# Windowed attention and expert choice on one core: one mask-and-maximum product for three blocks, and a single search over both halves of the key for the first list

## Chip, cores and metric

The kernel runs on 1 core of one Trainium2 chip. The metric is the device time of one execution in microseconds (us). The kernel before took 684.95 us, the median of three runs (682.93 to 686.85).

## The reference

Attention over 8 batches and 8 heads of 576 tokens, head size 64. Heads 0 to 3 see the last 32 positions, heads 4 to 7 every fourth of the last 128. Its result, 4608 tokens of 512 numbers, goes through a mixture of 8 experts: all (token, expert) logits are sorted, and each pair is accepted in that order while the token is free and the expert has under 576 tokens.

```python
scores = scale * np.matmul(q, k.transpose(0, 1, 3, 2))
scores = np.where(masks[None, :, :, :], scores, -1000000000.0)
scores = scores - np.max(scores, axis=-1, keepdims=True)
attn = np.exp(scores)
attn = attn / (np.sum(attn, axis=-1, keepdims=True) + 1e-09)
x = np.matmul(attn, v)            # as (B*S, H*D)
logits = x @ w_gate
order = np.argsort(-logits.flatten())
for idx in order:
    tok, e = (int(idx) // E, int(idx) % E)
    if assigned[tok] >= 0 or counts[e] >= cap:
        continue
    assigned[tok] = e
    counts[e] += 1
for e in range(E):
    out[assigned == e] = np.maximum(x[assigned == e] @ w1[e], 0.0) @ w2[e]
```

## The kernel before

**Attention.** There are 32 units: batch b, kind (plain or dilated heads) and ui (a pair of heads). A unit has 9 blocks c of 64 queries, in two halves h of 32; a half sees 64 keys. `Unit.build` (L434) makes its work:
- `scan` (L491): the mask by a product with the identity (L494) and bf16 scores on top of it (L498), into a PSUM tile pm, in two groups of 5 and 4 blocks (`gr`, L423). DVE takes each row's maximum into mx (L445).
- The turn (L450): one product with the identity turns mx, so that 9 rows hold the maxima; DVE copies them as bf16 into rows 64 to 72 of the unit's tile in R (L452). The rows above hold fixed choosers (`rsel`, loaded by `choosers`, L363).
- `scores` (L501), three times three blocks: for each block and half one product of `lsel` (mask rows and -1 for the maximum) with R (L505, 73 rows, 64 columns), then the fp32 scores on top (L510). ACT takes the exponential into E (L464).
- `values` (L514): E times V (L522); `weigh` (L526) on DVE divides by the sums into xs. `banks` (L567) turns xs (L581) and ACT copies it into xt; per batch the gate's logits follow (L606, L627).

The work is not issued in program order: `Schedule` (L155) is given each operation's cost, dependencies and due time, and a planner writes down one order for each engine when the kernel is built. On the chip each engine takes its instructions in that order and waits for semaphores. All loads are issued on SP's queue and are held back until PE has come to a mark (`paced`, L317); the constants and the first unit's loads come first (L740 to L750).

**Lists.** `choose` (L927) makes, as tokens are finished, each token's largest logit, its expert (oh0) and a sortable key, of which V0 holds the upper 16 bits and `lo` the lower; `bits` (L933) writes the expert as a bit into who; `coarse` (L798) counts keys over 256 thresholds. An expert's list closes at the first key for which it has 576 tokens. `alone` (L949) finds this for the first list with no other work beside it: `search_alone` (L870) runs rounds of flags on DVE (L825, L827), counts of 36 chunks on PE (L892), the comparison with 576 (L905) and a product that hands the step to all rows (L906); twice over the upper half (the coarse counts spare two rounds), then `low` (L976) builds V2 from the found place (L908) and the lower half, and four rounds follow over V2. Then the expert's bit (L963), the number of tokens above the found key in each expert (`over`, L967), the flags of members (L972), `ranks` (L1070: sums over all rows and over earlier rows, L1074 and L1075), `expert` (L1018: one-hot, what is still open, and the index eidx for the loads), `need_of` (L1054: how many tokens of equal key fit), and `accept` (L1077: running sums L1082, places, acceptance). `slots` and `listing` (L1302) turn the places into a list of token numbers: digits on DVE (L1128), their product with the chunk number on GpSimd (`by_chunk`, L1132) and with the row number on ACT, and PE's placing (L1153); `indices` (L1156) makes idx.

**Experts.** Round r: GpSimd gathers the list's tokens from DRAM in five tiles (L1332), PE turns them (L1346), ACT and DVE split them into high and low parts, three products for each block form the hidden layer (L1383) and the output (L1426), GpSimd scatters the rows. The next lists (`search`, L1251; `settle`, L1276) are made beside it. `fetch` (L1461) reads eidx on SP, and behind it the expert's w1 blocks are loaded (L1226); from the fourth on they wait for a mark that GpSimd writes after the gathers (L1217).

## Time and profile before

| | us |
|---|---|
| median of 3 runs | 684.95 |
| the profiled execution | 684.68 |
| its span, first to last instruction | 682.7 |
| PE busy, PE weight loads | 627.5, 548.3 |
| DVE, ACT, GpSimd busy | 463.4, 295.1, 207.0 |

Columns of a row: start and duration in us, engine, source line, operation, written tile <- read tiles, size, count, and in brackets the engine's idle time ahead of it and what ended it. PE is the product, PEld its weight load, POOL is GpSimd, SPq the sequencer of the load queue. The view of busy time by stage gives PE, PEld, DVE, ACT and POOL in this order and ends its rows with PE's granted clock (1.00 is full), the busy share of the 16 DMA engines and GB/s. A busy PE is not a PE at its peak, since products overlap. In the chain of work that ended last PE has 54% of the span, DVE 18%, and 15% is "issue", time for which the profile names no releaser.

### The profile page before, as it was taken

To read this page: it belongs to the slowest core of one execution; us is meant where nothing else is said; L and a number is where in the kernel's file an instruction comes from. 1 tells how busy PE (TensorE), PEld (TensorE's weight loads), DVE (VectorE), ACT (ScalarE), POOL (GpSimd) and SP (SyncE) were. 2 spreads that over 40 slices of the span, in tenths; PEclk is the share of its full clock that TensorE was granted. 3 is DMA by queue.
4 is the path that set the end of the run, shared out by engine and by line. 5 is a ranking of instruction groups with operands and counts; after the bars stand their busy time and mean duration, and the time that the engine had idled before them with its cause. 6 is when DMAs were issued, how large, how long until landed. Compare 5 with 4: busy or idle time off the path is not lost.

```text
span 682.7 us, 19041 instructions
## 1 busy us (share of the span) xinstructions
PE 627.5 (92%) x7514; PEld 548.3 (80%) x7514; DVE 463.4 (68%) x1576; ACT 295.1 (43%) x644; POOL 207.0 (30%) x316
## 2 busy tenths in 40 slices
PE   7889886789856999999999999999999999999994
PEld 5777776678644988998799799889879979988983
DVE  6677756876677885689798598778869736614200
ACT  5645453455403835855345145335423526424210
POOL 5465566552004217524113113110320311311011
PEclk9999999999957999999999999999999999999998
DMA  8998798872204937967236117214513644202001
GB/s 245 281 270 261 186 254 246 242 203 69 73 1 153 237 66 202 275 142 252 92 96 208 42 56 228 90 55 139 178 48 88 238 170 147 70 31 102 1 28 42
DMA packets 51674, 99.10 MB, mean 145 GB/s; under 512 B 7168, under 2 KB 17152, under 8 KB 51584
## 3 DMA queue, kind: packets, MB, share of 16 engines
q1 hardware_dynamic: 42240, 72.71, 35.5%
q0 software_dynamic: 9344, 25.17, 13.4%
q8 instruction: 59, 0.97, 0.6%
q14 instruction: 31, 0.25, 0.1%
HBM read 72.69 MB, written 18.87 MB: 134 GB/s over the span
## 4 chain that ended last, share of the span: by engine, by line
PE 54%; DVE 18%; issue 15%; DMA 5%; POOL 4%; ACT 2%; POOLq 0%; SPq 0%; DVEq 0%; ACTq 0%
PE ph L1383 16%; PE py L1426 16%; PE px L522 4%; PE pS L510 3%; PE px L581 2%; DVE xs L532 2%; PE ptx L1346 2%; POOL xg L1332 1%; DVE hb L1404 1%; POOL out L1452 1%; PE pz L813 1%; DVE mx L445 1%; DVE G L827 1%; PE py L1429 1%; PE py L1431 1%
## 5 line engine op out<-in xcount | busy, mean ns | idle before, releaser
L1426 PE MATMUL py<-w2h,hb 128*128 128x512 f32 x512 | 170.5, 398 | 0.0
L1383 PE MATMUL ph<-xh,w1h 128*128 128x256 f32 (+1 forms) x512 | 138.3, 301 | 0.0
L1383 PE MATMUL ph<-xh,w1l 128*128 128x256 f32 (+1 forms) x512 | 136.3, 297 | 0.0
L1383 PE MATMUL ph<-xl,w1h 128*128 128x256 f32 (+1 forms) x512 | 136.1, 296 | 0.0
L1426 PEld LDWEIGHTS py<-w2h,hb 128*128 128x128 f32 x512 | 96.1, 188 | 19.1
L1208 ACT ACTIVATE hb<-ph 128x256 fp32r<-128x256 f32 (+2 forms) x192 | 59.7, 346 | 102.4 <-PE ph L1383 100.5
L1452 POOL DMA_INDIRECT out<-y,idx x40 | 40.4, 1011 | 209.2 <-ACT y L1208 145.5
L1426 PE MATMUL py<-w2l,hb 128*128 128x512 f32 x256 | 99.8, 390 | 0.0
L1383 PEld LDWEIGHTS ph<-xh,w1h 128*128 128x128 f32 x512 | 91.7, 189 | 0.6
L1383 PEld LDWEIGHTS ph<-xl,w1h 128*128 128x128 f32 x512 | 91.6, 189 | 0.0
L1383 PEld LDWEIGHTS ph<-xh,w1l 128*128 128x128 f32 x512 | 91.5, 190 | 0.0
L1404 DVE SCALAR_TENSOR_TENSOR hb<-ph,hb 128x320 fp32r<-128x320 f32 (+1 forms) x128 | 57.1, 453 | 34.1 <-ACT hb L1208 30.6
L464 ACT ACTIVATE E<-pS 128x384 f32<-128x384 f32 x96 | 46.1, 490 | 54.3 <-PE pS L510 49.2
L1208 ACT ACTIVATE y<-py 128x512 f32<-128x512 f32 (+1 forms) x40 | 23.9, 597 | 96.0 <-PE py L1426 83.2
L510 PE MATMUL pS<-q,k 128*64 128x64 f32 x1152 | 54.2, 230 | 4.6 <-issue 4.6
L1426 PEld LDWEIGHTS py<-w2l,hb 128*128 128x128 f32 x256 | 48.2, 188 | 8.5
L1332 POOL DMA_INDIRECT xg<-xd,idx x40 | 41.6, 1039 | 36.3 <-PE ph L1383 26.2
L522 PE MATMUL px<-v,E 128*64 128x65 f32 x1152 | 47.7, 224 | 4.5 <-issue 2.2
L522 PEld LDWEIGHTS px<-v,E 128*64 128x64 f32 x1152 | 42.1, 138 | 8.4 <-issue 4.8
L297 POOL COPY v<-v 32x520 f32<-32x520 f32 (+2 forms) x56 | 33.4, 620 | 50.3 <-DMA v<-in_vd 20.7
L1209 DVE TENSOR_TENSOR xl<-ptx,xh 128x512 fp32r<-128x512 f32 (+1 forms) x36 | 22.9, 636 | 36.7 <-ACT xh L1208 28.7
L510 PEld LDWEIGHTS pS<-q,k 128*64 128x64 f32 x1152 | 45.3, 141 | 2.9 <-issue 2.9
(203 smaller groups left out, 1118.7 us busy)
## 6 DMA issues: line engine op xcount, KB each, us to landing
raw<-in_moe_w SPq DMA_DIRECT2D x128, 256.0 KB
qs<-in_qp SPq DMA_DIRECT2D x16, 288.0 KB
k<-in_kp SPq DMA_DIRECT2D x16, 288.0 KB
qs<-in_qd SPq DMA_DIRECT2D x16, 288.0 KB
k<-in_kd SPq DMA_DIRECT2D x16, 288.0 KB
xd<-xs SPq DMA_DIRECT2D x8, 512.0 KB
w2l<-raw POOLq DMA_DIRECT2D x16, 256.0 KB
v<-in_vp SPq DMA_DIRECT2D x8, 325.0 KB
```

The costliest lines, as they stand in the source:

```text
L297: f(t[:32, c0 + 1:c1 + 1], t[96:, c0:c1])
L464: e = self.op("ACT", 490, lambda j=j, pS=pS: nc.scalar.activation(self.E[:, 3 * j:3 * j + 3].rearrange("p c x -> p (c x)"), pS.tile[:, :38 ...
L510: x = nc.tensor.matmul(pS[64 * h:64 * h + 64, k, :, h], self.K[:, 32 * g:32 * g + 64], self.Q[:, g], start=False, stop=True, skip_group_ch ...
L522: x = nc.tensor.matmul(px[64 * h:64 * h + 64, c - c0, a], self.E[:, k, 64 * a:64 * a + 64], self.V[:, k, 2 * self.ui + a], start=True, sto ...
L532: nc.vector.tensor_tensor(xs[:, c0:c1, 2 * self.ui:2 * self.ui + 2], px[:, :m, :, :D], rc[:, :, :, None].to_broadcast([128, m, 2, D]), op= ...
L1208: act = lambda o, i, f=AF.Copy: nc.scalar.activation(o, i, f)
L1209: sub = lambda e, o, a, b: e.tensor_tensor(o, a, b, op=OP.subtract)
L1332: nc.gpsimd.indirect_dma_start(out=xg[:n], out_offset=None, in_=xd, in_offset=bass.IndirectOffsetOnAxis(ap=box[0][:n, m:m + 1], axis=0))
L1383: nc.tensor.matmul(o, a[:, d * 128:d * 128 + 128], b[:, d, c0:c1], start=((d, i) == pairs[0]), stop=((d, i) == pairs[-1]))
L1404: hl = op("DVE", 335 if j == 0 else 400, lambda: nc.vector.scalar_tensor_tensor(hb[:, CAP + c0:CAP + c1], o, 0.0, hb[:, c0:c1], op0=OP.max ...
L1426: nc.tensor.matmul(py, x, w, start=(f + i == 0), stop=(f == NF - 1 and i == 2))
L1452: s = nc.gpsimd.indirect_dma_start(out=out, out_offset=bass.IndirectOffsetOnAxis(ap=box[0][:n, m:m + 1], axis=0), in_=y[:n], in_offset=None)
```

## The change

*Attention.* `lsel` and `rsel` are laid out anew: three blocks stand in rows 0 to 95 and the nine maxima in rows 96 to 104, so that one product of 192 columns for each half (instead of three of 64) gives mask and maximum of three blocks. For that the maxima are written into three column sets of a wider mx, turned by three products, and copied (9 rows, 384 wide) into the wider R by ACT instead of DVE. The groups of the maxima become 6 and 3 blocks. R is loaded in two parts, one for each kind, from one copy in DRAM; mask tables are a third smaller.

*First list.* `search_alone` becomes one loop of six rounds: in its fourth the step is handed on in units of 65536 and X = 65536 (V0 - base) + lo replaces V0, so that found and `low` go. `bits` of the last five chunks moves from the attention's end into a round of that loop. `over` and `need_of` go; need is 576 less the last running sum (`accept`). A third product in `ranks` with -1024 on the diagonal makes the place of accepted tokens negative, in place of an addition. In the first list the product with the chunk number runs on DVE, between the digits, not on GpSimd; `named` (the open experts and eidx) is split off `expert` and put behind the last digits, and the fetch of eidx with the w1 loads behind it follows. The copies for the next search (`copies`) wait for the second gathered tile. Tiles of the gather and rx are touched ahead of the search.

*Later lists.* `count` counts once instead of twice, and `need_of` is gone.

The diff, cut to its core:

```diff
-        ls = np.zeros((128, NB, 64), np.float32)
+        ls = np.zeros((128, 3, 2, 64), np.float32)
-            ls[32 * h:32 * h + 32, c] = win
-            ls[64 + c, c] = -1.0
+            ls[32 * (c % 3):32 * (c % 3) + 32, c // 3, h] = win
+            ls[96 + c, c // 3] = -1.0
-    r = np.zeros((2, 32, 4, 2, 2, 32), np.float32)
-    for h in range(2):
-        r[h, :, :, h] = np.eye(32)[:, None, None, :]
-    bf["rsel"] = np.concatenate([r.reshape(64, -1), np.zeros((64, 512), np.float32)])
+    r = np.zeros((4, 32, 3, 2, 2, 32), np.float32)
+    for k in range(3):
+        r[k, :, k] = np.eye(32)[:, None, None, :]
+    bf["rsel"] = r.reshape(128, -1)
...
-    RS = pk.tile([128, 4, 128], BF, name="R")
+    RS = pk.tile([128, 4, 3, 128], BF, name="R")
-    MX, REC = ring(pk, [128, 64], BF, "mx", 3), ring(pk, [128, LG], F32, "rec", 3)
+    MX, REC = ring(pk, [128, 256], BF, "mx", 3), ring(pk, [128, LG], F32, "rec", 3)
...
-    def choosers():
+    def choosers(kind):
         c0, w = load_const.where["rsel"]
-        return nc.sync.dma_start(RS.rearrange("p x i -> p (x i)"), T["in_cb"][:, c0:c0 + w])
+        return nc.sync.dma_start(RS[:, 2 * kind:2 * kind + 2].rearrange("p x k i -> p x (k i)"),
+                                 T["in_cb"][:, None, c0:c0 + w].to_broadcast([128, 2, w]))
...
-            self.gr, self.gv = ((0, 5), (5, 9)), ((0, 3), (3, 5))
+            self.gr, self.gv = ((0, 6), (6, 9)), ((0, 3), (3, 5))
...
-                d = self.op("DVE", 80 * (c1 - c0), lambda c0=c0, c1=c1, pm=pm: nc.vector.tensor_reduce(
-                    mx[:, c0:c1], pm.tile[:, :64 * (c1 - c0)].rearrange("p (c j) -> p c j", j=64), axis=AX.X, op=OP.max),
+                d = self.op("DVE", 170 + 64 * (c1 - c0), lambda c0=c0, c1=c1, pm=pm: nc.vector.tensor_reduce(
+                    mx[:, 32:227].rearrange("p (k x) -> p x k", x=65)[:, c0:c1:3],
+                    pm.tile[:, :64 * (c1 - c0)].rearrange("p (j k x) -> p j k x", k=3, x=64), axis=AX.X, op=OP.max),
...
-            t = self.op("PE", 60, lambda: nc.tensor.matmul(pm.tile[64:, :128], mx, C["ident"], start=True, stop=True), md, B_A)
+
+            def turn(pm=pm):
+                for k in range(3):
+                    nc.tensor.matmul(pm.tile[64:, 128 * k:128 * k + 128], mx[:, 64 * k:64 * k + 64], C["ident"],
+                                     start=True, stop=True, skip_group_check=True)
+
+            t = self.op("PE", 150, turn, md, B_A)
             usem.append(t)
-            rc = self.op("DVE", 290, lambda: nc.vector.tensor_copy(self.r[64:64 + NB], pm.tile[64:64 + NB, :128]),
-                         [t, ready["r"], *old("r", kind, ui)], B_A)
+            o = self.r[96:96 + NB].rearrange("p k x -> p (k x)")
+            deps = [t, ready["r", kind], *old("r", kind, ui)]
+            rc = self.op("ACT", 500, lambda: act(o, pm.tile[96:96 + NB, :384]), deps, B_A)
...
         def scores(self, j, pS):
             pS = pS[:, :384].rearrange("p (c a h i) -> p c a h i", c=3, a=2, h=2)
-            for k in range(3):
-                for h in range(2):
-                    nc.tensor.matmul(pS[64 * h:64 * h + 64, k, :, h], self.ls[:64 + NB, 3 * j + k], self.r[:64 + NB, 64 * h:64 * h + 64],
-                                     start=(k == 0), stop=False, skip_group_check=True)
+            for h in range(2):
+                nc.tensor.matmul(pS[64 * h:64 * h + 64, :, :, h], self.ls[:96 + NB, 2 * j + h], self.r[:96 + NB, :, 64 * h:64 * h + 64],
+                                 start=True, stop=False, skip_group_check=True)
...
-        un.op("DVE", 350, lambda: R.bits(c0 - 1, c1), [x], B_P)
...
-    ready["r"] = sp(1, choosers, (), 131000, 0)
+    ready["r", 0] = sp(1, lambda: choosers(0), (), 197000, 0)
     load(0, 0, 1)
     load_values(0, 0)
+    ready["r", 1] = sp(1, lambda: choosers(1), (), 197000, 0)
     load(0, 1, 0)
...
+        big, V65 = (pw.tile([128, n], d, name=x, bufs=1) for n, d, x in ((128, BF, "unit65"), (NCH, F32, "V65")))
+        nc.scalar.activation(big, C["unit0"], AF.Copy, scale=float(NK))
+        nc.scalar.activation(self.down, C["ident"], AF.Copy, scale=-1024.0)
...
+        V, kb, base = self.V0, self.kstep(2, False), None
+        for it in range(2, 8):
+            w = kb.shape[1]
+            ps = self.pz[:w, 420:420 + NE]
...
-                self.flags(V, psc if it else None, kt, c0, c1)
+                self.flags(V, psc, kb, c0, c1)
                 for c in range(c0, c1):
                     nc.tensor.matmul(ps, self.G[:, c, :w], oh[:, c], start=(c == 0), stop=(c == NCH - 1))
+            b = pw.tile([128, 1], F32, name="base")
+            if base is None:
+                nc.vector.tensor_copy(b, psc)
+            else:
+                nc.vector.tensor_scalar(b, psc, base, 65536.0 if it == 3 else -1.0 if it == 7 else 0.0,
+                                        op0=OP.add, op1=OP.mult if it == 3 else OP.add)
+            base = b
+            if it == 2:
+                nc.vector.tensor_scalar(V65, V, 65536.0, None, op0=OP.mult)
+            if it == 3:
+                V = self.X = pw.tile([128, NCH], F32, name="X")
+                nc.vector.scalar_tensor_tensor(V, V65, base, self.lo, op0=OP.subtract, op1=OP.add)
+                kb, base = self.kstep(0, True), None
+            elif it < 7:
+                kn = self.kstep((it + 1) % 4, it > 3)
                 kb = pw.tile([128, NK + 1], F32, name="kb")[:, :kn.shape[1]]
                 nc.vector.tensor_scalar(kb, kn, base, None, op0=OP.add)
+            if it == 5:
+                self.bits(NCH - 5, NCH)
             flag = pw.tile([NK + 1, 1 + NE], BF, name="flaga")
             nc.vector.tensor_scalar(flag[:w, 1:], ps, float(CAP), None, op0=OP.is_ge, op1=OP.max, accum_out=flag[:w, :1])
-            nc.tensor.matmul(self.pa[:, :1 + NE], C[f"unit{it}"][:w], flag[:w], start=True, stop=True)
...
+            nc.tensor.matmul(self.pa[:, :1 + NE], (big if it == 3 else C[f"unit{it % 4}"])[:w], flag[:w], start=True, stop=True)
+        self.delta, self.base = psc, base
...
-        self.search_alone(self.V, self.oh, False)
-        self.low()
-        self.search_alone(self.V2, self.oh, True)
+        self.search_alone()
...
-        s = pw.tile([n, 1], F32, name="sa")
-        nc.vector.tensor_scalar(s, self.C["kpos"][:n, 1:], self.delta[:n], None, op0=OP.is_equal)
-        pr = pw.tile([n, NE], F32, name="pra")
-        nc.vector.tensor_scalar(pr, self.ps, s, None, op0=OP.mult)
-        self.over = self.pa[:, 16:16 + NE]
-        nc.tensor.matmul(self.over, self.C["onesf"][:n], pr, start=True, stop=True)
-        self.above()
+        gg = pw.tile([128, 2, NCH], BF, name="gg")
+        for w, o in ((0, OP.is_gt), (1, OP.is_equal)):
+            nc.vector.tensor_scalar(gg[:, w], self.X, self.delta, self.base, op0=OP.subtract, op1=o)
+            if w == 0:
+                bit = pw.tile([128, 1], I32, name="bit")
+                nc.vector.tensor_reduce(bit, self.fe, axis=AX.X, op=OP.max)
...
+        self.em = em
+
+    def named(self):
+
+        nc, pw, em = self.tc.nc, self.pw, self.em
...
-        nc.tensor.matmul(ps[:, 2 * NCH:], C["tri"], ge, start=True, stop=True)
+        nc.tensor.matmul(ps[:, 2 * NCH:], C["tri"], ge, start=True, stop=False, skip_group_check=True)
+        nc.tensor.matmul(ps[:, 2 * NCH:3 * NCH], self.down, ge[:, :NCH], start=False, stop=True, skip_group_check=True)
...
-        pre = self.pre = pw.tile([128, 2, NCH], F32, name="pre")
+        need = pw.tile([128, 1], F32, name="need")
+        nc.vector.tensor_scalar(need, scan[:, 0, NCH - 1:], -1.0, float(CAP), op0=OP.mult, op1=OP.add)
+        pre = pw.tile([128, 2, NCH], F32, name="pre")
         nc.vector.tensor_tensor(pre, ps[:, 2 * NCH:].rearrange("p (w c) -> p w c", w=2), scan, op=OP.add)
+        slot = self.slot = pw.tile([128, NCH], F32, name="slot")
+        nc.vector.scalar_tensor_tensor(slot, pre[:, 1], need, pre[:, 0], op0=OP.min, op1=OP.add)
         acc = self.acc = pw.tile([128, NCH], F32, name="acc")
-        nc.vector.scalar_tensor_tensor(acc, pre[:, 1], self.need, ge[:, 1], op0=OP.is_lt, op1=OP.mult)
-        nc.vector.tensor_tensor(acc, acc, ge[:, 0], op=OP.add)
+        nc.vector.scalar_tensor_tensor(acc, pre[:, 1], need, ge[:, 1], op0=OP.is_lt, op1=OP.mult)
...
-    def by_chunk(self, c0, c1):
+    def by_chunk(self, c0, c1, first):
+        if first:
+            pair = lambda x: x.rearrange("p c (x t) -> p c x t", t=2)
+            n = self.C["ctab"][:, 2 * c0:2 * c1].rearrange("p (c t) -> p c t", t=2)
+            return self.tc.nc.vector.tensor_tensor(
+                pair(self.rx[:, c0:c1, 0]), pair(self.oa[:, c0:c1]),
+                n[:, :, None, :].to_broadcast([128, c1 - c0, NM, 2]), op=OP.mult)
...
+    for x in XG.tiles:
+        nc.gpsimd.memset(x[:1, :1], 0.0)
     R.alone()
...
-            nd = st["need"] = chain("DVE", 310, R.need_of, [], B_L)
-            nd = st["need"] = chain("DVE", 310, R.need_of, [m, st.get("slots")], B_L)
...
-            oc = chain("ACT", 1055, lambda: R.copies(R.oh, nc.scalar), [lv])
+            st["left1"] = lv
+            oc = chain("ACT", 1055, lambda: R.copies(R.oh, nc.scalar), [lv]) if r else None
...
+        if r:
+            rows(*halves[0])
+        for k, n in enumerate(OB[r > 0]):
             c0, c1 = c1, c1 + n
-            lows.append((op("DVE", 100 + 36 * n, lambda c0=c0, c1=c1: R.within(c0, c1), [d], B_L), c0, c1))
-        halves = [(0, 14), (14, NCH)] if r == 0 else [(0, NCH)]
-        xs = [(op("POOL", 150 + 30 * (c1 - c0), lambda c0=c0, c1=c1: R.by_chunk(c0, c1), [d], B_L),
-               op("ACT", 250 + 9 * (c1 - c0), lambda c0=c0, c1=c1: R.by_row(c0, c1), [d], B_L)) for c0, c1 in halves]
+            if r == 0 and k < 2:
+                rows(*halves[k])
+            deps = [xs[-1][0]] if r == 0 else [d]
+            lows.append((op("DVE", 100 + 36 * n, lambda c0=c0, c1=c1: R.within(c0, c1), deps, B_L), c0, c1))
+        if r == 0:
+            st["named"] = op("DVE", 350, R.named, [lows[-1][0]], B_L + 5000)
...
+        if r == 0:
+            st["fetch"] = EN[r] = get(st["named"])
+        en = EN[r]
         X[r] = gather(r, ix, BOX[r])
+        if r == 0:
+            st["next"][0] = chain("ACT", 1055, lambda: R.copies(R.oh, nc.scalar), [st["left1"], X[0][1][0]])
```

## Rows read from the trace of the kernel before

**Rows 1.** busy time by stage: stretch, its us, each engine's busy us (count)

```profile
0.00:188.00 188.00, 158.31 (x4064) 135.82 (x4064) 133.29 (x439) 96.27 (x205) 93.66 (x161) 1.00 0.76 212
20.00:68.00 48.00, 43.41 (x1179) 38.34 (x1180) 33.09 (x107) 28.11 (x62) 28.45 (x45) 1.00 0.92 270
68.00:119.00 51.00, 39.75 (x1157) 36.24 (x1157) 33.66 (x110) 22.89 (x48) 31.68 (x52) 1.00 0.88 231
188.00:218.50 30.50, 17.69 (x306) 12.82 (x307) 23.16 (x100) 4.79 (x8) 7.11 (x8) 0.61 0.19 57
218.50:660.00 441.50, 437.56 (x3086) 388.44 (x3085) 306.90 (x1039) 192.27 (x428) 103.16 (x142) 1.00 0.43 128
```

**Rows 2.** PE's waits, 68 to 119 us: us, times, longest

```profile
PE pS L510 <- issue: 4.6, 4, 1.4
PE pS L505 <- issue: 3.6, 4, 2.0
PE px L522 <- ACT E L464: 0.8, 1, 0.8
PE pm L494 <- DVE R L452: 0.8, 1, 0.8
PE px L522 <- issue: 0.8, 1, 0.8
```

**Rows 3.** busy time between restarts of PE, columns as in rows 1

```profile
68.75:118.82 50.07, 39.58 (x1148) 36.07 (x1148) 33.66 (x110) 22.89 (x48) 30.80 (x50) 1.00 0.88 231
108.87:114.25 5.38, 3.85 (x128) 3.65 (x128) 4.19 (x12) 2.72 (x5) 3.25 (x6) 1.00 1.03 244
```

**Rows 4.** DMA queues, 106 to 107.6 us: packets, MB, share

```profile
q8 instruction: 1, 0.02, 4.0%
```

**Rows 5.** timeline of PE, 29 to 30 us

```profile
29.09 0.30 PE L494 MATMUL pm<-const 128*64 128x256 bf16 x2
29.22 0.29 PE L498 MATMUL pm<-k,q 128*64 128x64 bf16 x8
29.34 0.26 PE L505 MATMUL pS<-R,const 73*64 73x64 bf16 x6
29.44 0.55 PE L510 MATMUL pS<-q,k 128*64 128x64 f32 x12
```

**Rows 6.** groups by line, 0 to 187 us: busy us, mean ns, idle

```profile
L464 ACT ACTIVATE E<-pS 128x384 f32<-128x384 f32 x96 | 46.1, 490 | 54.3 <-PE pS L510 49.2 <-PE pm L450 4.7
...
L452 DVE CAST R<-pm 9x128 bf16<-9x128 f32 x32 | 9.3, 289 | 10.3 <-PE pm L450 8.8 <-PE px L522 0.9
```

**Rows 7.** DVE's waits, 0 to 188 us

```profile
DVE R L452 <- PE pm L450: 8.8, 13, 1.4
```

**Rows 8.** chain of work that ended last, 0 to 20 us: start, us, what

```profile
13.13 5.55 DMA v<-in_vd
```

**Rows 9.** timeline of DVE and PE, 194 to 206 us

```profile
194.24 0.22 DVE L908 TENSOR_SCALAR found<-py,base 128x1 f32<-128x1 f32 x1 [0.26 <-PE py L906]
...
195.22 0.90 DVE L825 TENSOR_TENSOR G<-V,const 128x224 bf16<-128x224 f32 x3
...
203.28 0.22 DVE L908 TENSOR_SCALAR found<-py,base 128x1 f32<-128x1 f32 x1 [0.26 <-PE py L906]
203.41 0.22 DVE L959 SCALAR_TENSOR_TENSOR fe<-py,const 128x8 f32<-128x8 f32 x1
...
204.75 0.25 PE L1075 MATMUL pz<-ge,const 128*128 128x72 bf16 x1
...
205.61 0.29 DVE L1082 TENSOR_TENSOR_SCAN scan<-const,pz 128x72 f32<-128x72 f32 x1
```

**Rows 10.** timeline of all engines, 206 to 216 us

```profile
206.69 1.48 SPq L1226 DMA_DIRECT2D raw<-in_moe_w  x3
...
211.45 1.45 POOL L1332 DMA_INDIRECT xg<-xd,idx  x1 [2.20 <-DVE idx L1165]
...
215.31 0.66 PE L1346 MATMUL py<-const,xg 128*128 128x128 f32 x4 [0.84 <-DMA xg<-xd,idx]
```

114 lines of the change are left out of this document (47 added, 67 removed).

## The prediction

> **What bounds the kernel now.** I read the busy time by stage first, to see where PE has idle time that an edit could give back. From 218.5 us on PE is busy 437.56 of 441.50 us [rows 1]: there an edit on another engine is worth nothing, but whatever makes that stretch begin earlier moves the end by as much. Two stretches ahead of it are open: the attention (up to 188 us, PE busy 158.31), and the lone search for the first list (188 to 218.5 us), where PE is busy 17.69 of 30.50 us and the instructions wait for each other one by one.
>
> Inside the attention I read PE's waits of 68 to 119 us. PE is busy 39.75 of 51 us there [rows 1], and 9.0 us of its waits, nine of them, stand under "issue", with no releaser; E and the copy into R hold it 0.8 us each [rows 2]. What the nine are shows in a window cut from one such restart to the next: it holds exactly 128 products and 128 weight loads, 256 instructions, and takes 5.4 us, in which PE is busy 3.85 [rows 3]. The DMA view just ahead of the first of these restarts (108.87 us) shows one packet of the instruction queue [rows 4]. So I read PE as waiting for the next 256 of its own instructions. The 50.07 us from 68.75 to 118.82 hold 1148 and 1148 of them [rows 3], nine blocks.
>
> The Trainium skill's Runtime: NRT & Kernel Launch, section Instruction fetch mechanics, has instructions come in blocks of 256 and says that the cost of crossing a block's edge is mostly hidden. The block's size agrees with rows 3, the hiding does not. By the page's rule the waits would have another cause and fewer instructions would give nothing, which is the first rival below.
>
> **Part 1, attention.** (a) *Scores.* Six mask-and-maximum products in each third of a unit become two with 192 columns. Six run in 29.44 - 29.34 = 0.10 us; a pair of 256 columns, one in each half of the array, takes 29.22 - 29.09 = 0.13 us [rows 5], so a pair of 192 takes 0.08 to 0.10. PE gains 0 to 0.02 us in each of 96 thirds, 0 to 1.9 us; I take 0, because the columns are the same.
> (b) *Instructions.* A unit has 18 such products; they become 6, and one turn of the maxima becomes three: 10 products and 10 loads fewer, 20 of a unit's 254 (4064 + 4064 up to 188 us, over 32 units [rows 1]), 7.9%. Where PE waits for blocks, time goes with their number: 7.9% of 50.07 us is 3.9 us. Bounds: 0, if something else is late at once, and -4.5 with a few such waits elsewhere. I take -3.5, a little under the whole, because the waits there (9.0 us) are over twice that and the transfers have room: 231 GB/s against 270 from 20 to 68 us [rows 1].
> (c) *Two more turns a unit*, 128 columns each: 0.05 us apiece at the pitch of rows 5 (0.13 us for 256), 32 x 0.10 = 3.2 us in all. In the block-bound stretch the wait hides them (some 9 units); of the other 23 about half lie on PE's path. Bounds 0 and +3.2; I take +1.1.
> (d) *The copy into R* goes from DVE (0.289 us, 32 times) to ACT, three times as wide. The nearest ACT row is the exponential of 128x384, 0.49 us [rows 6], so about 0.5 us, 16 us of ACT in all; ACT is busy 96.27 of 188 us [rows 1]. DVE loses 9.2 us of work and also the 8.8 us in which it stood before this copy, 13 times, until PE had turned the maxima [rows 7]; the weighing and the next maxima were queued behind it. ACT now stands there, with exponentials and the copies of Q and XT behind it, and PE's second product waits for the exponentials. PE itself waited 0.8 us for the copy in 51 us [rows 2], 2.9 us over 188; I take -1.2, under half, because the copy itself is longer on ACT. Bounds: -9.2 (all that DVE loses of work) and +8.4 (the third rival).
> (e) *Maxima.* 5 + 4 blocks become 6 + 3 with the same elements: 0.
> (f) *Constants.* R grows from 128 KB to twice 192 KB, both mask tables shrink by 48 KB: 160 KB more ahead of the first V of the second kind, and the chain runs through that load (5.55 us from its issue [rows 8]). At 270 GB/s [rows 1]: +0.6 us; bounds 0 (hidden) and +0.8.
> Sum: -3.5 + 1.1 - 1.2 + 0.6 = **-3.0 us**.
>
> **Part 2, the first list.** (a) *One search.* The second half's first flags start when PE's answer comes (194.24 us, where L908 starts), not at 195.22 [rows 9]: -0.98 us. V65, X and the bases run while PE counts. (b) *bits* of the last blocks moves into a later round: two instructions of some 0.2 us (the nearest is L908's 0.22 [rows 9]), where DVE waits for PE only a part of that: +0.3, bounds 0 and +0.4; where it was, DVE waited for PE anyway, so nothing comes back. Both: -0.7; bounds -1.0 and -0.5.
> (c) *Tail.* found, s, pr and their product go, and *need* comes from the running sums. Before, the sums (L1082) start at 205.61 us, 2.33 us after PE's answer (203.28), though PE's ranks ended at 205.00 (L1075: 204.75 + 0.25) [rows 9]: DVE was late, with the index and need_of. After: three instructions fewer ahead of the ranks, at a pitch of 0.13 us, the distance of L908 and L959 [rows 9]: -0.4; one more small product, +0.05; then the sums start 0.26 us behind PE, DVE's wait in L908's row. 205.00 - 0.4 + 0.05 + 0.26 = 204.91: -0.7. *need* and the dropped addition cancel.
> (d) *GpSimd out.* Two DVE products of 140 and 220 elements, about 0.2 us each, one of them ahead of the first digits; it takes the place of GpSimd's, for which PE's placing waited before: 0, bounds -0.3 and +0.3. (e) The first gather's instruction takes 1.45 us [rows 10]; a part of that may be the first use of the tiles, now touched early: -0.1, bounds -0.5 and 0.
> Gather earlier by 0.7 + 0.7 + 0.1 = 1.5 us.
> (f) *Index behind the list.* named() moves behind the last digits, some 0.4 us that PE's placing hides. The SP queue fetches the index after it, so the first three w1 blocks (768 KB), issued from 206.69 us on, well ahead of the first gather at 211.45 [rows 10], come at about the gather's own time. On SP only w1's other blocks are queued behind them, and those wait for the gathers anyway. PE needs w1 only when the gathered tokens are turned (from 215.31 us [rows 10]) and split, so its own lateness costs 0; but 768 KB take 2.8 us at 270 GB/s, beside the gathers' first 512 KB (1.9 us). Bounds: 0, and +1.9 if both gathers wait as long as they take themselves; I take +0.6, a third, since both queues move at once. (g) The copies for round 1 go behind the second tile, off the path.
> Sum: -1.5 + 0.6 = **-0.9 us**.
>
> **Part 3, later rounds.** need_of goes, one small product a list comes. PE is full: at most +0.3 us; I take 0.
>
> **Rivals.** *The blocks give nothing*: another limit (transfers, busy 0.88 of that stretch) holds PE as long, and the wait only changes its name. For it: that share. Against: 270 GB/s were moved just before. Then the attention gives +0.5 (b = 0) and the list -0.9: 684.68 - 0.4 = 684.3 us.
> *DVE was the brake*: without the copy half of its bound arrives, 4.6 us instead of 1.2: 684.68 - 3.9 - 3.4 = 677.4 us. Against: from 68 to 119 us DVE is busy 33.66 of 51.
> *ACT becomes the gate* (slower). A copy that PE waits for costs its 0.5 us and the mean wait that DVE had before it, 8.8 / 13 = 0.7 us, 1.2 together, in place of the 1.2 gained by (d). It decides from about 5 of 32 units on: 684.68 - 2.7 + 5 x 1.2 is 3.3 us over the run before. With 7, half of the 13: 684.68 - 2.7 + 8.4 = 690.4 us. For it: ACT takes its work in order and gets 16 us more. Against: ACT is busy about half, and PE waited for E once in rows 2.
>
> **How the numbers follow.** The profiled execution took 684.68 us (a span of 682.7 and 2 around it), 0.3 under the median of 684.95, so its rows stand for the runs: 684.68 - 3.0 - 0.9 = **680.8 us**. Chances: forecast 0.60 (own range 678 to 683), blocks give nothing 0.20, DVE 0.08, ACT 0.12. A measurement of this kernel tells about 0.5% (3.4 us) from no change, so faster means under 681.5: 0.42 of the forecast's 0.60, and DVE's 0.08, together 0.50. Slower: 0.11 of ACT and 0.02 of the first rival, 0.13. The rest, 0.37, is within 0.5%. The range leaves out ACT's case and a part of DVE's: 676.5 to 686.
>
> **What would show it.** Right: the experts' first product about 4 us earlier; PE's "issue" waits of that stretch down from 9.0 us to about 6, with more of a unit in a block of 256; DVE's waits for the turn gone, and ACT's before the copy short; no gap between the two halves of the search, and the sums some 1.4 us sooner. Wrong: PE waiting for E; "issue" waits as long as before; the tokens' first turn not earlier, behind the w1 blocks.

## The result and the profile after

| | us |
|---|---|
| kernel before, median of 4 | 684.18 (682.93 to 686.85) |
| changed kernel, median of 4 | 693.36 (690.22 to 695.08) |
| ratio | 1.0109 (95%: 1.0071 to 1.0147) |
| forecast | 680.8 (676.5 to 686) |

The change makes the kernel 1.1% slower; the forecast had the wrong sign and its range doesn't hold the time. Ratios, here and below, leave out disturbed executions (up to four of six, in `a_start`), so they are not always the quotient of the medians; differences in us are the ratio's distance from 1 times the median of before beside it. The profiled execution of the changed kernel took 690.22 us (span 688.3), its fastest: the profile shows 5.5 of the 9.2 us.

Busy time by stage, changed kernel, columns and stretches of [rows 1]:

```profile
0.00:188.00 188.00, 157.68 (x3698) 134.76 (x3703) 122.43 (x394) 109.76 (x235) 94.81 (x161) 0.96 0.74 210
20.00:68.00 48.00, 42.35 (x1013) 37.00 (x1015) 28.36 (x91) 30.09 (x64) 25.99 (x41) 0.93 0.87 239
68.00:119.00 51.00, 42.88 (x1044) 37.70 (x1040) 33.40 (x108) 30.52 (x68) 32.46 (x51) 0.97 0.88 248
188.00:218.50 30.50, 17.54 (x334) 12.76 (x331) 23.09 (x106) 3.28 (x10) 3.48 (x8) 0.61 0.17 50
218.50:660.00 441.50, 435.96 (x3088) 387.24 (x3089) 309.03 (x1029) 193.46 (x431) 104.41 (x143) 1.00 0.42 129
```

PE has 9% fewer products up to 188 us (the change takes away 7.9%; the rest come later than 188 us, since the attention ends later), DVE 11 us less and ACT 13.5 us more work. But PE's granted clock in the attention is 0.96 where it was 1.00, and the attention's last keys come at 191.65 us, before at 187.09. What was forecast inside it mostly came about. PE's waits of 68 to 119 us, to be set beside [rows 2]:

```profile
PE pS L518 <- issue: 2.4, 2, 1.7
PE px L530 <- issue: 2.1, 1, 2.1
PE px L614 <- issue: 2.1, 1, 2.1
```

"issue" fell from 9.0 to 6.6 us there. The copy into R, from the groups by line, 0 to 192 us:

```profile
L286 ACT ACTIVATE R<-pm 9x384 bf16<-9x384 f32 x32 | 15.5, 483 | 13.9 <-PE pm L455 6.9 <-PE px L530 2.4 <-issue 1.5
```

And PE's waits for it, same stretch (us, times, longest):

```profile
PE pS L513 <- ACT R L286: 0.8, 2, 0.6
```

0.48 us each, as estimated, and PE waits for it 0.8 us in the whole attention: ACT's copy is no gate. The list's part, timeline of all engines, beside [rows 9] and [rows 10]:

```profile
198.56 1.09 DVE L836 SCALAR_TENSOR_TENSOR G<-X,py,const 128x224 bf16<-128x224 f32 x3 [0.26 <-PE py L924]
...
206.80 0.23 DVE L974 SCALAR_TENSOR_TENSOR fe<-py,const 128x8 f32<-128x8 f32 x1 [0.26 <-PE py L924]
...
208.03 0.23 PE L1082 MATMUL pz<-ge,down 128*128 128x36 bf16 x1
...
208.29 0.30 DVE L1089 TENSOR_TENSOR_SCAN scan<-const,pz 128x72 f32<-128x72 f32 x1
...
213.66 1.48 SPq L1245 DMA_DIRECT2D raw<-in_moe_w  x3
...
214.63 1.13 POOL L1362 DMA_INDIRECT xg<-xd,idx  x1 [20.38 <-DVE Lt L1072]
...
219.45 0.91 PE L1376 MATMUL py<-const,xg 128*128 128x128 f32 x4 [2.25 <-DMA xg<-xd,idx]
```

The second half's flags follow PE's answer after 0.26 us, without a gap; the sums start 0.26 us behind the last rank's product. From the first flags (190.19 us before, 194.50 after) to the sums it was 15.42 us and is 13.79. Little of that reaches the experts: from the first flags to the first turn of gathered tokens it was 25.12 us (to 215.31) and is 24.95 (to 219.45).

What the forecast has no step for stands at the start, PE's timeline:

```profile
17.66 0.39 PE L507 MATMUL pm<-k,q 128*64 128x64 bf16 x12
20.86 1.76 PE L589 MATMUL px<-const,xs 128*128 128x128 f32 x10 [2.81 <-DMA const<-in_cf]
22.55 0.37 PE L503 MATMUL pm<-const,const 128*64 128x192 bf16 x2
```

PE turns xs (L589) before it has finished the next unit's maxima (L503), and waits 2.8 us for the identity of that turn to land; the third unit's last exponential starts at 26.74 us instead of 22.21, the fourth's at 31.29 instead of 24.80. In the kernel before, the maxima came first and the same wait was 1.05 us; in `att` and `aft`, which have the changed kernel's order and are described below, it is 2.60 and 2.13. Nothing in the diff moves these operations: the planner did, from the new costs and load sizes.

### The profile page after: what moved, and what is told of

Read it like the earlier page. It is cut to its first block, busy times and chain, and to the rows that moved or that the text cites. A ratio compares the mean times of both kernels' runs of the same rounds, so it can differ in the third digit from the quotient of the medians.

```text
span 688.3 us, 18430 instructions
## 1 busy us (share of the span) xinstructions
PE 630.7 (92%) x7201; PEld 550.6 (80%) x7203; DVE 454.6 (66%) x1528; ACT 308.9 (45%) x679; POOL 207.4 (30%) x319
## 4 chain that ended last, share of the span: by engine, by line
PE 53%; DVE 17%; issue 15%; DMA 8%; POOL 3%; ACT 3%; POOLq 0%; SPq 0%; DVEq 0%; ACTq 0%
PE ph L1413 16%; PE py L1456 16%; PE px L530 3%; DMA raw<-in_moe_w 3%; PE pS L518 3%; PE px L589 2%; PE ptx L1376 2%; PE pz L822 1%; DVE hb L1434 1%; DVE xs L540 1%; DMA v<-in_vd 1%; DVE G L836 1%; POOL out L1482 1%; PE py L1459 1%; DVE mx L446 1%
## 5 line engine op out<-in xcount | busy, mean ns | idle before, releaser
L530 PE MATMUL px<-v,E 128*64 128x65 f32 x1152 | 49.8, 227 | 4.3 <-issue 4.1
L518 PEld LDWEIGHTS pS<-q,k 128*64 128x64 f32 x1152 | 48.8, 143 | 4.2 <-issue 4.2
L530 PEld LDWEIGHTS px<-v,E 128*64 128x64 f32 x1152 | 43.9, 140 | 8.2 <-issue 6.3
```

What stands on the lines that cost most here:

```text
L518: x = nc.tensor.matmul(pS[64 * h:64 * h + 64, k, :, h], self.K[:, 32 * g:32 * g + 64], self.Q[:, g], start=False, stop=True, skip_group_ch ...
L530: x = nc.tensor.matmul(px[64 * h:64 * h + 64, c - c0, a], self.E[:, k, 64 * a:64 * a + 64], self.V[:, k, 2 * self.ui + a], start=True, sto ...
```

## Experiments: each part by itself

`att` is the change's attention part in the kernel before, `lst` its list part, `lst_early` the list part with the index named and fetched where it was. `bef_more` adds products to the kernel before:

```diff
+            if j == 0:
+                for _ in range(10):
+                    nc.tensor.matmul(pS[:64, 510:511], C["ident"][:, :64], C["ident"][:, :1], start=True, stop=True,
+                                     skip_group_check=True)
```

> The attention part of the change alone (constants, R, wider mx, three turns, copy on ACT, groups of 6 and 3); the lists are as before. The order of every engine within the attention is that of the changed kernel. My sum forecast -3.0 us. Theory 'start': the constants that come ahead of the first units, and a PE order that puts the first turning of xs ahead of other work, cost about 4 us by the third unit and the attention never gets them back: +4 to +5 us. Rival 'ACT': the copy of the maxima on ACT holds PE: also slower, but then the loss grows from unit to unit instead of standing at the third. Rival 'blocks' (my forecast's main term): faster by 3.

> The list part alone (single search, need from running sums, GpSimd out, index behind the list, later rounds); the attention is as before, but for bits of the last chunks. My sum forecast -0.9 us: gather about 1.5 earlier, and 0.6 of it lost to the w1 blocks beside it. Rival 'late index': the w1 blocks come with the gathers, these land 1 us later than their issue allows, PE's clock falls while it waits, and the experts' first products start later than before: 0 to +2 us.

> The list part alone, with one thing put back: the index of the first expert is named right after the search and fetched ahead of the list, as before the change, so that the first three w1 blocks move ahead of the gathers. If the late index costs something, this is faster than the list part alone by what it costs (0.6 by my sum, 1 to 3 by the rival 'late index'), less some 0.4 us that the three naming instructions take on DVE ahead of the sums. If the late index costs nothing, the two are the same or this one is 0.4 slower.

> The kernel before with 10 more products of one column and 10 loads in each unit (20 PE instructions, as many as the change removes), in the same planned order; their results go nowhere. By my step (b) PE's blocks of 256 instructions set the pace from 68 to 119 us, so that stretch takes 7.9% longer, +3.5 us (plus up to 0.15 us in each unit that they take on PE outside it, +3 at most). By the rival that the blocks give nothing: 0 to +1 us, the waits at the blocks' edges being a part of another limit.

Beside a kernel before of 690.03 us:

| | median | ratio (95%) | us |
|---|---|---|---|
| att | 694.60 | 1.0067 (1.0029 to 1.0106) | +4.6 |
| lst | 689.86 | 0.9982 (0.9946 to 1.0018) | -1.2 |
| lst_early | 692.72 | 1.0039 (1.0002 to 1.0076) | +2.7 |
| bef_more | 696.84 | 1.0061 (1.0022 to 1.0101) | +4.2 |

The attention part loses, against the forecast's -3.0; the list part is about where it was forecast (-3.7 to +1.2). The early index gains nothing, so the late one isn't the cause. 20 more PE instructions a unit cost 4.2 us (1.5 to 7.0) with every engine's order kept, as step (b) expects, but the 320 little products also keep PE busy themselves, so this doesn't single out the instruction blocks.

## Experiments: the attention alone

Attention scatters by several us, which drowns in 690. So the next kernels leave out lists and experts:

```diff
-        with ExitStack() as c2:
-            moe(tc, c2, C, R, xd, T["in_moe_w1"], T["in_moe_w2"], out)
+        tc.nc.sync.dma_start(out[:128, :NCH], R.V0)
```

`a_bef` is that cut of before, `a_att` of `att`. `a_start` repairs the start of `a_att`: the turn depends on the load it reads, which has its old size in the planner:

```diff
-        ready["c", i] = sp(1 if i < 3 else 3, lambda: load_const(i), (), 128 * (1408, 768, 1920, 3200)[i], 0)
+        ready["c", i] = sp(1 if i < 3 else 3, lambda: load_const(i), (), 128 * (1408, 768, 1920, 4500)[i], 0)
...
-            t = un.op("PE", 109 * (c1 - c0), turn, [*(done if b < B - 1 else done[:i + 1]), *oldt], late, pt, 128)
+            t = un.op("PE", 109 * (c1 - c0), turn, [*(done if b < B - 1 else done[:i + 1]), *oldt, ready["c", 3]], late, pt, 128)
```

`a_ord` has all of the attention's change but the copy on ACT, and the planner keeps the costs of before (also those of the maxima, the scores and the constants), which gives every engine the order of before:

```diff
-            t = self.op("PE", 150, turn, md, B_A)
+            t = self.op("PE", 60, turn, md, B_A)
-            rc = self.op("ACT", 500, lambda: act(o, pm.tile[96:96 + NB, :384]), deps, B_A)
+            rc = self.op("DVE", 290, lambda: nc.vector.tensor_copy(o, pm.tile[96:96 + NB, :384]), deps, B_A)
...
```

> The attention of the kernel before up to the last key, alone: lists and experts are left out, and one small store of the keys ends it. It is the measure for the three kernels beside it, whose loss must then show against some 195 us instead of 690. Expected of every theory: 187 to 191 us to the last key and some 4 us around it, 191 to 196 us.

> The same cut (lists and experts left out) with the whole attention part of the change. If the loss of 4.6 us that this part showed in the whole kernel lies in the attention, it is 3 to 6 us slower than the same cut of before. If it lies behind it (the experts starting with a late clock or a late transfer), 0 or below: by the forecast -3.0.

> The cut of the attention part with one repair: the turning of xs is made to depend on the load of the identity it uses, and that load keeps its old size in the planner, so that PE has the third unit's maxima ahead of the turning again and doesn't stand there for 2.8 us. Theory 'order' (the loss comes from the order that the new costs gave, at the start above all): within 1 us of the cut of before, 3 us or more below the attention part's cut. Rival 'ACT' (the wide copy on ACT is late for PE all the way): as slow as the attention part's cut, 3 to 6 us over before. Rival 'start is hidden': the third unit comes 4 us earlier and the end doesn't.

> The cut of the attention part with the copy into R on DVE and the planner given the old costs, so that every engine has its work in the order of before; only the products (20 PE instructions a unit fewer), the wider copy and the larger R differ. Theory 'order': faster than the cut of before by the forecast's terms without the move of the copy, -3.5 + 1.1 + 0.6 and up to +1 for the wider copy, so -2 to 0 us. Rival 'products' (masks of three blocks and two more turns cost more than their columns): 3 us or more slower.

Two more followed. `a_ident` is `a_att` with the identity's 64 KB loaded earlier and every engine's order kept; `a_ordact` is `a_ord` with the copy issued on ACT at the same place:

```diff
-        for t, src in parts[i:i + 1] if i < 3 else parts[3:]:
+        for t, src in parts[i:i + 1] if i < 2 else parts[2:4] if i == 2 else parts[4:]:
```

> The cut of the attention part (lists and experts left out) with every engine's order as in that cut; only the 64 KB identity that the turning of xs waits for at 17.9 us is loaded earlier, right behind the second kind's maximum tables. Beside a kernel before of 685.7 us the cuts took 193.2 (before), 195.1 (attention part) and 187.1 (repaired). Theory 'wait' (the 2.8 us at the start and what follows from them are the loss): 187 to 190 us. Rival 'order' (the repair changed PE's order in all units after it, and that is what counts): 194 to 196 us.

> The cut with the order of before on all engines (191.9 us with the copy into R on DVE), and the copy now issued on ACT at the same place of the order. It is the move of the copy by itself. The forecast's step: -1.2 us, so about 190.7. Rival 'ACT becomes the gate': 3 to 8 us more, 195 to 200. If ACT's place is the only matter and half of what DVE loses arrives: 187.

Ratios are to the whole kernel before (685.66 us beside the first four, 685.16 beside the last two); the last column is the difference of the ratios times 685.5, each uncertain by about 1.5 us:

| | median | ratio (95%) | us against a_bef |
|---|---|---|---|
| a_bef | 193.24 | 0.2793 (0.2775 to 0.2810) | |
| a_att | 195.10 | 0.2854 (0.2839 to 0.2868) | +4.2 |
| a_start | 187.14 | 0.2697 (0.2680 to 0.2713) | -6.6 |
| a_ord | 191.91 | 0.2782 (0.2768 to 0.2795) | -0.8 |
| a_ident | 193.35 | 0.2813 (0.2803 to 0.2823) | +1.4 |
| a_ordact | 189.81 | 0.2773 (0.2762 to 0.2784) | -1.4 |

(The expectations speak of differences of medians: by these `a_ordact` is 3.4 below, `a_att` 1.9 above.) PE's timeline in `a_start`:

```profile
18.15 0.36 PE L507 MATMUL pm<-k,q 128*64 128x64 bf16 x11 [0.43 <-ACT R L286]
...
20.09 0.36 PE L455 MATMUL pm<-const,mx 128*64 128x128 bf16 x3 [0.50 <-DVE mx L446]
...
22.00 0.77 PE L589 MATMUL px<-const,xs 128*128 128x128 f32 x5
```

The turn of xs now stands behind the third unit's maxima and finds its identity there. So: the same instructions take 10.8 us less (`a_att` to `a_start`; 8.0 by the medians) when the planner is told that the turn needs the identity. `a_ident`, in whose trace PE no longer waits there, takes back 2.8 of these (1.8 by the medians); that is the wait itself. The rest is the order, of the start and of all units behind it, since one changed time sets the planner on another way. The work of the change, with each engine in its old order, is worth -1.4 (`a_ordact`; -0.8 without the copy's move): the forecast's direction, with less than its -3.0 by the ratios, and within the 1.5 us by which each difference is uncertain. Theory "order" stands, theory "products" falls, and "ACT becomes the gate" falls too: at a fixed order the move of the copy gained 0.6 by the ratios and 2.1 by the medians.

The "issue" waits don't follow the number of instructions: up to 180 us they add up to 5.8 us in `a_bef`, 1.3 in `a_ord`, 5.3 in `a_ordact`, 6.8 in `a_att` and 12.8 in `a_ident`, the last two with the same PE instructions in the same order.

## Experiments: behind the attention

`aft` is the changed kernel again, `fix` the changed kernel with the repair of `a_start`.

> The changed kernel, all of it, beside the others on this chip. The attention part alone gave +4.6 and the list part alone -1.2 on one chip, both together +9.2 on another. If the parts add up: before + 2 to + 5 us. If they disturb each other (the loads of the first expert behind a late attention): before + 7 or more.

> The changed kernel, all of it, with the one repair of the start (the turning depends on the identity's load, which keeps its old size in the planner). If the 6 us that the cut gained against the cut of before reach the experts, and the list part gives its 1: before - 5 to - 8 us. Rival 'given back': the experts begin as late as before, within 1.5 us of before.

`aft` took 694.43 us, ratio 1.0130 (1.0101 to 1.0160), +8.9; `fix` 685.56, ratio 1.0000 (0.9974 to 1.0026). The parts don't add up: `att` and `lst` make +3.4 together, the whole kernel +8.9, the second case of the expectation. The repair is worth 8.9 us, but it only brings the kernel level: attention (-6.6) and list (-1.2) should have put it some 8 below. That is the number of the rival 'given back', not its mechanism: in `fix` the experts' first hidden block begins at 212.53 us, before at 218.54. In the trace of `aft` the time is lost in the first two experts; its first flags come at 188.75 us, ahead of the 190.19 of the kernel before (the same kernel's first profile has them at 194.50, so single profiles of the attention scatter by as much as the start is worth). ACT's timeline around the second expert's gathered tiles:

```profile
269.71 0.60 ACT L1227 ACTIVATE xh<-ptx 128x512 fp32r<-128x512 f32 x1 [1.93 <-PE ptx L1376]
273.96 0.63 ACT L1227 ACTIVATE w1h<-raw 128x512 fp32r<-128x512 f32 x1 [3.65 <-DMA raw<-in_moe_w]
274.62 0.63 ACT L1254 ACTIVATE w1l<-w1h 128x512 fp32r<-128x512 f32 x1
275.15 0.58 ACT L1227 ACTIVATE xh<-ptx 128x512 fp32r<-128x512 f32 x1
```

DVE's, same place:

```profile
275.77 0.69 DVE L1228 TENSOR_TENSOR xl<-ptx,xh 128x512 fp32r<-128x512 f32 x1 [4.73 <-ACT xh L1227]
```

PE's:

```profile
271.61 0.60 PE L1376 MATMUL ptx<-const,xg 128*128 128x128 f32 x4
...
273.67 0.40 PE L1461 MATMUL py<-w2l,hb 128*64 128x512 f32 x1
276.51 0.66 PE L1376 MATMUL ptx<-const,xg 128*128 128x128 f32 x4 [2.45 <-DVE xl L1228]
```

Read from the bottom: PE needs ptx free, which DVE's xl frees, which needs ACT's xh. PE had turned that tile by 272.21 us (271.61 + 0.60), but ACT stands for 3.65 us at w1h, the split of a weight block that is still on its way, and xh is behind it in its queue. ACT's queue in the kernel before, at the same place:

```profile
271.83 0.60 ACT L1208 ACTIVATE xh<-ptx 128x512 fp32r<-128x512 f32 x1 [1.92 <-PE ptx L1346]
...
274.12 0.60 ACT L1208 ACTIVATE xh<-ptx 128x512 fp32r<-128x512 f32 x1 [0.30 <-PE ptx L1346]
274.61 0.62 ACT L1208 ACTIVATE w1h<-raw 128x512 fp32r<-128x512 f32 x1
```

There the tile goes first and w1h finds its block. Some 23 us later it happens to w2 in `aft`, through three engines. ACT's timeline:

```profile
297.00 0.63 ACT L1227 ACTIVATE w2h<-raw 128x512 fp32r<-128x512 f32 x1 [3.08 <-DMA raw<-in_moe_w]
297.54 0.53 ACT L1227 ACTIVATE hb<-ph 128x320 fp32r<-128x320 f32 x2
```

DVE's:

```profile
298.10 0.49 DVE L1434 SCALAR_TENSOR_TENSOR hb<-ph,hb 128x320 fp32r<-128x320 f32 x1 [3.71 <-ACT hb L1227]
```

PE's:

```profile
300.65 0.64 PE L822 MATMUL pz<-G,ohr 128*128 128x64 bf16 x9 [3.18 <-DVE G L836]
```

The search's flags G are queued on DVE behind hb. All kernels with the list part have this order on ACT (their planner has new costs for the lists; which of them sets it was not tried), none without it. PE's waits for xl and G in the second expert are 2.5 to 8.6 us in the profiles of the six kernels with this order (`after`, the profile shown first, 2.5, `aft` 5.6, `lst` 8.6) and 0.7 to 2.1 in the five with the lists of before. Four kernels tell what it is worth. `fix_x` is `fix` with the splits put behind the tiles again:

```diff
+        behind = X[1][4 if n == "2" else 3][0] if r == 1 and (n == "2" or f >= 4) else None
-        hi = op("ACT", 525, lambda: act(h, raw), [ld, *oldh, st["rows"] if first else None], B_W)
+        hi = op("ACT", 525, lambda: act(h, raw), [ld, *oldh, st["rows"] if first else behind], B_W)
```

`fix_early` is `fix` with the index early, as in `lst_early`; `start` and `ordact` are `a_start` and `a_ordact` as whole kernels, with the lists of before.

> The attention part alone in the whole kernel, with the repair of the start (the turning depends on the identity's load, which keeps its old size in the planner); lists and experts as before. Theory 'experts': the 7 us that the repaired whole kernel lost behind the attention come with the list part (it changes what stands ahead of what in ACT's queue for the second expert), so without it the cut's -6 arrives: before - 4 to - 7 us. Rival 'given back anyway' (an earlier end of the attention meets loads of the experts that come no earlier): within 2 us of before.

> The attention part in the whole kernel, every engine in the order of before (the copy into R issued on ACT at the same place), lists and experts as before. Its cut gave -3.4 us against the cut of before (and -1.3 with the copy left on DVE). The forecast's own sum for this part was -3.0. Theory: before - 2 to - 4.5 us. Rival 'given back anyway': within 1.5 us of before.

> The changed kernel with the repaired start, and in the second expert ACT's splits of w1 and w2 put behind the copies of the gathered tiles again, as they stood before. In the changed kernel ACT stood 3.65 us for the load of w1 with the third tile's copy behind it, and PE 2.8 us for that copy. Theory 'ACT's queue': 2 to 4 us under the same kernel without this (which was level with before, 685.2 to 685.6), so before - 2 to - 4. Rival 'loads' (the weights come late anyway, and the wait goes to the first hidden block): within 1 us of before.

> The changed kernel with the repaired start, and the first list's index named and fetched ahead of the list's digits again, so that three w1 blocks are issued some 7 us ahead of the first gather as before. Theory 'late index' (768 KB less have come when the experts begin, and the first two experts run at the pace of their loads): 2 to 4 us under the repaired kernel, before - 2 to - 4. Rival 'ACT's queue': the order of the second expert stays, so no gain, within 1 us of before; the earlier naming itself costs the list up to 0.5 us.

Last, `aft_x` is `aft` with ACT's order alone repaired, `fix_xe` has both repairs and the early index.

> The changed kernel with ACT's splits in the second expert behind the gathered tiles' copies again, and its start left as it is. The changed kernel was 9.3 us over before; with the start repaired level with before; with both repaired 9.2 under. If the two losses are separate, this one stands 6 to 8 us under the changed kernel: before + 1 to + 4 us. If the late start is the whole matter and ACT's order hurts only beside it: before + 7 or more.

> Both repairs and the first list's index named and fetched early as before, so that ACT's order no longer stands between the index and the time. With both repairs and the late index the kernel was 9.2 us under before (interval - 12.3 to - 3.3 by the ratio). Theory 'the late index costs nothing': before - 6 to - 9. Rival 'late index': 2 us or more under that, before - 10 to - 12.

Beside a kernel before of 690.95 us (first four) and 686.52 (last two):

| | median | ratio (95%) | us |
|---|---|---|---|
| start | 685.31 | 0.9930 (0.9888 to 0.9973) | -4.8 |
| ordact | 690.29 | 1.0006 (0.9968 to 1.0043) | +0.4 |
| fix_x | 681.77 | 0.9887 (0.9822 to 0.9952) | -7.8 |
| fix_early | 686.83 | 0.9971 (0.9936 to 1.0005) | -2.0 |
| aft_x | 689.29 | 1.0020 (0.9981 to 1.0058) | +1.4 |
| fix_xe | 678.60 | 0.9872 (0.9816 to 0.9929) | -8.8 |

By the ratios ACT's order is worth 7.8 us with the start repaired (`fix` 0.0, `fix_x` -7.8; uncertain by some 5) and 7.5 without (`aft` +8.9, `aft_x` +1.4; by some 3.5). But `fix` and `aft` ran beside a kernel before of 685.16 us, `fix_x` and `aft_x` beside 690.95 and 686.52; by the medians alone it is 3.8 and 5.1, and `fix_early` and `fix_x`, which ran side by side, are 5.1 apart (5.8 by the ratios). So it is 4 to 8 us, where 2 to 4 were expected of `fix_x`. The start is worth 9.2 with ACT repaired and 8.9 without (7.5 and 8.9 by the medians). Within these bounds the two losses are separate and add up, as `aft_x` was to show. `fix_x` and `fix_xe` beat both kernels. Between these two, and between `fix` and `fix_early`, the early index makes no difference that the intervals show.

PE's waits agree with ACT's order as the cause: 0.6 to 1.6 us for xl and G in the three kernels with ACT's repair. The repair moves some of ACT's other work too (copies of hidden blocks now stand ahead of w2h), and ACT still waits 3.31 us for w2 in `aft_x`; which of the moves counts was not tried. Open is also why `lst`, with the same order on ACT, measures -1.2: its profile, of its longest execution (698.43 us), shows the waits, its median does not. `start`, with the old lists and ACT's old order, kept its gain, as theory 'experts' says.

ACT's timeline in `fix_x`:

```profile
267.81 0.60 ACT L1227 ACTIVATE xh<-ptx 128x512 fp32r<-128x512 f32 x1 [1.93 <-PE ptx L1377]
...
270.10 0.60 ACT L1227 ACTIVATE xh<-ptx 128x512 fp32r<-128x512 f32 x1 [1.21 <-DVE xl L1228]
270.59 0.62 ACT L1227 ACTIVATE w1h<-raw 128x512 fp32r<-128x512 f32 x1
```

Busy time by stage of the first two experts in `aft`, each from its first product to the next one's:

```profile
216.50:279.30 62.80, 59.71 (x427) 52.53 (x425) 41.53 (x151) 35.10 (x73) 23.05 (x29) 0.99 0.72 192
279.30:344.90 65.60, 62.06 (x465) 54.56 (x463) 51.26 (x194) 31.00 (x68) 19.86 (x27) 0.95 0.57 150
```

The same in `fix_x`:

```profile
213.10:272.20 59.10, 58.89 (x428) 52.03 (x426) 41.86 (x152) 33.15 (x69) 21.09 (x28) 1.00 0.73 191
272.20:334.00 61.80, 59.67 (x465) 51.94 (x463) 51.27 (x194) 33.35 (x72) 21.73 (x29) 1.00 0.65 173
```

128.4 us against 120.9, with the same products: the waits, and PE's granted clock, which fell to a mean of 0.95 in the second stretch. A mean of 0.95 is a tenth of 65.6 us at the lower level (1.2 of 2.4 GHz), so some 3 us of work lost, by this estimate. In the profile shown first (690.22 us) the same two stretches took 122.0 us, in `fix` 123.6, in `lst` 129.7, in `aft_x` 120.6, in the kernel before 120.2: how long ACT stands depends on when the block lands, and a single profile can show little of it.

`ordact` stays open: its cut gained 1.4 and the whole kernel nothing (interval -2.2 to +3.0). Its trace has the last keys 2.5 us ahead of the kernel before's profile, and then a wait of 2.1 us for the first list's fourth gathered tile and a clock of 0.97 in the first expert. `start`, which kept its gain, has such a wait too (2.19 us, clock 1.00), so the wait alone doesn't explain it.

## Why the prediction was wrong

**The failed step is one that isn't there.** The description of the kernel, put down with the prediction, says that a planner orders the work from costs, dependencies and due times. The prediction then prices every edit at the order of before: a change of order stands in its sum at nothing, without a reason. The diff changes a dozen of the planner's numbers. In the attention this cost 4.2 + 1.4 = 5.6 us over the work at a fixed order (`a_att` against `a_ordact`), and 10.8 (8.0 by the medians) over the order that the repaired start gives; in the second expert 4 to 8. Both are larger than any term of the sum.

*Part 1 (a) scores, 0:* right; a pair of 192 columns takes 0.09 us (84.22 to 84.31 us), as estimated. *(e) maxima, 0:* right (64 of 456 ns, before 64 of 457 in the cut).

*(b) instructions, -3.5, and (c) turns, +1.1:* "issue" of that stretch fell to 6.6 us, about the 6 foretold, and the time was spent in other waits. At a fixed order (b), (c), (f) and the copy three times as wide on DVE gave -0.8 where the terms and that copy make -1.8 to -0.8. So the sum holds within 1.5 us, but its parts are not shown: "issue" varied tenfold between kernels with nearly the same instructions, so a price per instruction was not to be had from one profile. By the rule of the Trainium skill's Runtime: NRT & Kernel Launch, section Instruction fetch mechanics, that crossing a block's edge is mostly hidden, (b) would be 0 and the sum here +1.7 to +2.7. The -0.8, uncertain by 1.5, speaks against that rule here, as far as (c) was sized right.

*(d) copy, -1.2:* fits (-0.6 by ratios, -2.1 by medians, uncertain by 1.5), and its bound +8.4 was the wrong fear: ACT's copy took 0.48 us and PE waited for it twice.

*(f) constants, +0.6:* the term that was mis-sized. It counted the bytes, right, but the same line tells the planner when the identity lands: 3200 for 4500. The kernel gave the turn no dependence on that load, so only the planned times could keep it behind; in the changed kernel it stands ahead of the third unit's maxima. `a_start` restores the size and adds the dependence together, so which of the two the order needs is not separated. A size that a planner reads is an edit of order.

*Part 2 (a) to (c), -1.4:* right: -1.63 from first flags to sums. *(e) tiles touched early, -0.1:* the first gather's instruction took 1.13 us instead of 1.45, but not for that reason: in `lst_early`, `fix_early` and `fix_xe`, which touch the tiles too and name the index early, it takes 1.45 again. *(d) GpSimd out, 0, a miss:* from the sums to the gather it was 5.84 us and is 6.34. The gather starts 0.87 us behind the end of idx, before 0.29. The profile names the close's subtraction (213.99 us) as what released it; with the early index it names a weight split instead, at the same distance of 0.88, so neither is shown to be the reason. In all nine kernels with the list part GpSimd had stood idle for 20 us by then, in the others for 2.2; that would fit the product taken off it, but was not tried.

*(f) late index, +0.6:* no time shows it (`fix_xe`, `fix_early`, and `lst_early` with the other sign), but the traces do: from the first flags to the first turn of gathered tokens the six profiles with the late index take 24.65 to 25.22 us, the three with the early one 24.35 to 24.37, so it costs 0.3 to 0.9. Of the 25.12 us before, the list part as it stands therefore takes away 0.5 at most, where the forecast has 0.9. *(g), 0:* not tried by itself.

*Part 3, 0:* wrong by 4 to 8 us, for the whole of the expert stretch. "PE is full" [rows 1] was read as "an edit elsewhere is worth nothing". PE was full because ACT's queue happened to have the tiles ahead of late weights. The Trainium skill's PSUM — Partial Sum Buffer, section Engine vs sequencer instructions, has ACT's, DVE's and GpSimd's queues strictly first in, first out; the trace agrees: in `aft` the tile was turned by 272.21 us, and its xh began at 275.15, behind w1h.

*Rivals.* Slower came, but not by the mechanism of "ACT becomes the gate": it decided by waits for R, and those were 0.8 us. The true one is also a queue of ACT, at a place where no edit was made. "The blocks give nothing" and "DVE was the brake" don't describe it either. Once the orders are mended the kernel gains 7.8 us, further than the -3.9 forecast, but that is not the forecast come true: of the attention's -6.6 the work at the order of before makes -1.4, and in the whole kernel at that order nothing shows (`ordact`). The rest is an order that the planner happened to find.

## What to carry to other kernels

Where a planner writes the order, a diff of costs, sizes or engines is first a diff of orders: set the planned order of each engine beside the old one, and look for an instruction that waits for a load and now stands ahead of one that doesn't. Give such an instruction its real dependence, or a place behind the work that is ready, before pricing anything else. To price the work itself, hold the order fixed by giving the planner the old numbers; to see a few us in a kernel that scatters by as much, time the stage alone.

## What the runs showed of the hardware that was not expected

Of two waits of PE close in length one cost more than itself. In `aft` the granted clock was 1.00 before, during and behind the wait of 2.45 us that ended at 276.51 us. In the wait of 3.18 us that ended at 300.65 it fell, to 0.50 (1.2 of 2.4 GHz) from 300 to 306 us, and was back at 1.00 from 308 on, with PE busy all the time since the wait: some 3 us of work. And PE's "issue" waits are no fixed price: the same PE instructions in the same order, once with the identity's 64 KB earlier, had 6.8 us of them in one profile and 12.8 in the other.
